# Spread the making of w_down blocks, make the first gate/up block earlier, and remake the even blocks: two FNet and GEGLU layer pairs on one core

## The chip, the cores and the metric

The kernel runs on one core of one Trainium2 chip. The metric is the device time in microseconds of one execution, the median of the runs. Lower is better.

## The reference

Activations are 2048 rows (S) by 512 columns (D); the hidden width F is 1792. The pair of layers runs twice, with the same weights:

```python
def _A_ref(x, dft_seq_re, dft_seq_im, dft_hid_re, dft_hid_im):
    a = jnp.einsum("bsd,ed->bse", x, dft_hid_re)
    b = jnp.einsum("bsd,ed->bse", x, dft_hid_im)
    y = jnp.einsum("ts,bse->bte", dft_seq_re, a) - jnp.einsum("ts,bse->bte", dft_seq_im, b)
    return y

def _B_ref(x, w_gate, w_up, w_down):
    return (_gelu(x @ w_gate) * (x @ w_up)) @ w_down

x = A_x
x = x + _A_ref(_layernorm(x), ...)
x = x + _B_ref(_layernorm(x), ...)
x = x + _A_ref(_layernorm(x), ...)
x = x + _B_ref(_layernorm(x), ...)
```

## The kernel before

**Precision.** Every float32 operand is split into a high and a low float32r part: ScalarE copies the high part (line 128), VectorE subtracts it for the low part (line 130). A product is three matmuls, high by high, high by low, low by high (lines 174 to 176), 128 by 128 weights against 128 by 512 data.

**Fewer products.** The products are done by 2 by 2 block schemes with seven products in place of eight. Their operands are sums of blocks, named A11, A12, S1 to S4 and A22; VectorE makes the sums (`plus`, line 159, and `minus`, line 156).

**Layers 0 and 2** (`mix`) are the Fourier layers. The sequence matrix comes from memory as tiles of `ws`, in four row blocks of 512 rows, numbered 0 to 3. In layer 0 the A11 and A12 products of all four row blocks come first. Then follow, for each row block, the stage S2 (24 steps: the S2, S1 and S3 products) and the stage S4 (16 steps: S4 and A22), and the hidden-matrix products: for row blocks 0 and 1 one by one, for row blocks 2 and 3 together in a pair stage after the S4 stage of row block 3. A step is one call of `six` or of the like, six matmuls. At the end of S2 `plus(v, us[b][c], one[c])` reads two PSUM banks, and the S4 stage then accumulates into the same banks.

**Layers 1 and 3** (`geglu`) are the GEGLU layers, each in two halves `w` of 1024 rows. A half runs through 14 gate/up blocks (even numbers gate, odd ones up), `up(n)` for each, seven products and so seven steps; beside them run the A11 and A12 products with w_down of the blocks already done (`beside`), then the rest of the w_down products. A gate/up block is 512 KB of raw weights `wgu`. To *make* it is to load the raw weights (one load of 256 KB, two of 128 KB, lines 1072 to 1074), take four half-wide sums, split four pieces (3.5 splits), and store the parts to memory as seven tiles `wb` of 256 KB; later halves load the stored parts. `weight_steps` gives this as a `load` and five `runs` (the sums, four divisions). Blocks in `ANEW` are never stored and are made again in each later half. A w_down block (`wdc`, parts stored as `wc`) is made in the same way by `down_weight_steps`, and comes back by the stream of loads below; there are seven, of which the first two are made in layer 0.

**Who does what when.** One list `queue` holds small pieces of work; `step()`, called once per step, takes one of them. When `queue` is empty, `step()` takes one run from `spare`, which holds the w_down blocks' runs; `slow` is taken every few steps. In layer 0 the list `chores` of a row block is put into `queue` after the S4 stage of row block 2: the loads of gate/up blocks 0 and 1, the norms of the second half of the next layer's first 1024 rows, and the making of block 0. A norm loads a row tile of x in four pieces (`x_load_mixed`, line 215), takes its mean and variance on ScalarE and GpSimd (lines 549 to 554), normalizes it (line 579) and transposes it (line 670). Loads of `ws` and of stored parts are a stream: `take()` gives the next operand and loads and splits ahead of it, as far as the tiles in SBUF allow.

**Space and order.** SBUF is 93 slots of 128 by 512 floats, given out oldest first: a load into a slot waits until the last reader of what was there is done. The order of the instructions on each engine comes from a scheduler that starts from the order in which the program is written and moves instructions ahead of others where its own timing says so. On the chip every engine's queue runs in that order; loads are on SP's queue, stores on GpSimd's.

Of the kernel before, what the change touches and what calls it, by code (L numbers as in the profile page):

```python
# [18 lines left out]
NF = F // P  # L19
# [4 lines left out]
GELU_A = math.sqrt(2.0 / math.pi)  # L24
GELU_C = 0.044715
AHEAD = 7
MORE = 8
RAW = 6
WARM = 11
# [5 lines left out]
PACE = 9, 3  # L35
SKEW = 2, 1
NSLOT = 93
DOWN_FROM = 1
BEFORE = 2
ANEW = 3, 5, 7, 9  # L40
FORE = {0: 4, 2: 4}
MADE = 5
KEEP22 = {0: (), 2: ()}
PAIRED = {0: (2,), 2: (0, 2)}
# [19 lines left out]
def fnet_geglu(ctx: ExitStack, tc: tile.TileContext, x_in, ws, wh, whc, wgu, wdc, out):  # L64
# [226 lines left out]
    stream = {"loaded": 0, "split": 0, "used": 0, "more": 0}  # L291
# [24 lines left out]
        parts[n] = items[n][2](*raws.pop(n))  # L316
        stream["split"] += 1

    def brought_near():
        n = stream["used"]  # L320
        while stream["split"] < len(items):
            at = stream["split"]
            _, _, make, need = items[at]
            if too_far(at) or make is not whole and at > n + AHEAD + stream["more"]:
                break
            if make is not whole and need and need not in cs and at > n:
                break
            split_next()

    def take():  # L330
        n = stream["used"]
        brought_near()
        stream["used"] += 1
        return parts.pop(n)

# [96 lines left out]
    NP = NF // 2  # L432
# [63 lines left out]
                    items.append((F32R, (piece_of(wdd, k, name),), whole, near))  # L496


    queue, slow, spare, deferred, steps_done, pace = [], [], [], [], [0], [PACE[0]]

    def step():
        if queue:
            run = queue.pop(0)
            if run is not None:
                run()
        elif spare:
            spare.pop(0)()
            if len(spare) == 2 and down_making:
                load, runs = down_making.pop(0)
                load()  # L510
                spare.extend(runs)
        steps_done[0] += 1
        if deferred:
            deferred.pop(0)()
        elif slow and steps_done[0] % pace[0] == 0:
            slow.pop(0)()
# [217 lines left out]
    def mix(layer):  # L734
# [6 lines left out]
        def other_chores(b):  # L741
            if b == NB - 3:
                norms, others = block_steps(layer + 1, 0)
                later.update(norms=norms[NT:], fetches=others[:ND], others=others[ND:])
                return norms[:NT]
            if b == NB - 2:
                weights = [weight_steps(n) for n in range(2)] if layer == 0 else []
                norms = later.pop("norms")
                later["others"] += weights[1][1] if weights else []
                return [run for load, _ in weights for run in (load,)] + norms + (weights[0][1] if weights else [])  # L750
            return later.pop("others") if b == NB - 1 else []

        def hid_groups(b, groups):
# [91 lines left out]
        chains, sides, us, xrows, later = {}, {}, {}, {}, {}  # L845

        def plain_hid(b):
            return b not in PAIRED[layer] and b - 1 not in PAIRED[layer]
# [12 lines left out]
        def s2(b):  # L861
            last, fore = b == NB - 1, b < FORE[layer]
            if b == 0:
                lend("z")
                lend("x")
                if layer == 0:
                    pace[0] = PACE[1]
                    slow.extend(made_ahead())
            chain, one, three = chains.pop(b), [ps8.get() for _ in range(2)], [ps8.get() for _ in range(2)]
            sides[b] = one, three  # L870
            if last:
                queue.extend([run for fetch in later.pop("fetches") for run in (None, None, None, None, fetch)])
            for i, k in skewed(3):
                if plain_hid(b) and i == 0 and k == ROWS_AT:
                    xrows[b] = [x_load(layer, b * NT + n) for n in range(NT)]
                if b and fore and i == 0 and k == (0 if layer else BACK_AT):
                    cs.update({(0, c): fetched((layer, b, c, "sum"), True) for c in range(2)})
                if i == 0:
                    six(chain, "T2", k, False, k == NK - 1)
                elif i == 1:  # L880
                    six(one, "T1", k, k == 0, k == NK - 1, "T12" if last else None)
                else:
                    six(three, "T3", k, k == 0, k == NK - 1)
                if k < NK - 1:
                    continue
                if i == 0:
                    us[b] = [copied(p, True) for p in chain]
                    ps8.put(*chain)
                    if b in xrows:
                        seeds[b] = [seeded(t) for t in xrows[b]]  # L890
                        sb.put(*xrows.pop(b))
                for c in range(2):
                    if i == 1:
                        v = cs[1, 2 + c] = sb.get(own=True)
                        plus(v, us[b][c], one[c])
                        if plain_hid(b):
                            nc.scalar.activation(one[c], v, AF.Copy)
                    elif i == 2:
                        plus(cs[1, 2 + c], cs[1, 2 + c], three[c])
# [202 lines left out]
    def down_weight_steps(k):  # L1102
        return weight_steps(k, wdc, wdd)
# [10 lines left out]
            runs += [*todo[:2], *([after[0]] if after else []), *todo[2:]]  # L1114
        return runs

    down_making = []

    def piece_here(n, i, tiles):
        p = wparts.setdefault(n, {})  # L1120
# [24 lines left out]
    def geglu(w, layer):  # L1145
# [11 lines left out]

        making = {}
        if layer == 1 and w == 0:
            down_making.extend(down_weight_steps(k) for k in range(BEFORE, NP))  # L1160
            load, runs = down_making.pop(0)
            load()
            spare.extend(runs)
            making.update((n, weight_steps(n)) for n in range(2, NF))
            making[2][0]()
        else:
            making.update((n, weight_steps(n)) for n in ANEW)


        chain, side, c11, u, w4 = {}, {}, {}, {}, {}  # L1170
# [27 lines left out]

        def up(n):
            if layer == 1 and w == 0:  # L1200
                brought_near()
            if n + 3 in making:
                making[n + 3][0]()
            if n + 2 in making:
                first_run, *runs = making[n + 2][1]
                queue.extend([lambda: (first_run(), runs[0]()), *runs[1:]])
            product(n, chain[n], "S2", "T2", False, True)
            u[n] = copied(chain[n])
            down = beside(n)
            next(down, None)  # L1210
            side[n] = ps8.get()
            product(n, side[n], "S1", "T1", True, True)
            w4[n] = copied(side[n])
            next(down, None)
            first(n + 1)
            product(n, chain[n], "S3", "T3", False, True)
            v = w4.pop(n)
            plus(v, v, chain[n])
            finished(n, 1, 1, v)
            sb.put(v)  # L1220
            next(down, None)
            product(n, side[n], "S4", "B22", False, True)
            v = u.pop(n)
            plus(v, v, side[n])
            ps8.put(side.pop(n))
            finished(n, 0, 1, v)
            sb.put(v)
            next(down, None)
            second(n + 1)
            product(n, chain[n], "A22", "T4", False, True)  # L1230
            ps = chain.pop(n)
            if n % 2 == 0:
                v = copied(ps)
                finished(n, 1, 0, v)
                sb.put(v)
            else:
                finished(n, 1, 0, ps)
            ps8.put(ps)
            for _ in down:
                pass  # L1240
# [3 lines left out]
        def pair_combined(k):  # L1244

            b11, b12, b21, b22 = h4[k] = [h.pop((2 * k + i, part)) for i in range(2) for part in range(2)]
            minus(b11, b12, b11)
            minus(b12, b22, b12)
            bs["A12", k] = split_slot(b21)
            if k < MADE:  # L1250
                second_made(k)
                fourth_made(k)
# [64 lines left out]
                if name == "S4":  # L1317
                    rows_done(layer, w * 2 + 1)

        def beside_at(j):  # L1320

            if layer == 1 and w == 0:
                return DOWN_FROM + j * (NF - DOWN_FROM) // (NF - 1)
            return j + 1

        def beside(n):

            for j in range(NF - 1):
                if beside_at(j) != n:
                    continue  # L1330
                k, other = divmod(j, 2)
                if other:
                    pair_combined(k)
                    yield from down_product("A12", k)
                    continue
                if k == NP - 1:
                    load_turned(layer, w * 2)
                bs["A11", k] = split_slot(h[2 * k, 0])
                yield from down_product("A11", k)

        straight = []

# [39 lines left out]
        if w == 0:  # L1382
            norms, others = block_steps(layer, 1)
# [194 lines left out]
```

## Time and profile before

| | before |
|---|---|
| runs shown | 1596.65, 1597.31, 1597.11 us; median 1597.11 us |
| profiled execution | 1594.51 us, span 1592.7 us |
| TensorE busy | 1579.0 us, 6976 matmuls |
| VectorE, ScalarE, GpSimd busy | 1256.5, 926.1, 247.9 us |
| granted clock, mean | 0.997 |
| moved | 405.02 MB, mean 254 GB/s |

The span runs from the first to the last instruction; what lies around it is 1.8 us. Layer 0 takes the span up to about 397 us, its third row block the stretch from 245 to 299 and its fourth that from 299 to 359; the first half of layer 1 begins at about 397. Rows of the profile name an instruction by engine, line of the kernel, operation, tiles written and read, and times are microseconds from the span's start; names such as `s`, `p` and `wide` are slots, PSUM banks and the wide tile, without their numbers. A number in brackets is the time for which the engine was idle just before, with what ended it.

### The profile page before, as it was taken

The page shows a single profiled execution, that of the slowest core. Times are in us where ns is not written, and L with a number is a line of the kernel's source. Part 1 is how long each engine was busy: PE and PEld are TensorE (multiplying, and loading weights), DVE is VectorE, ACT ScalarE, POOL GpSimd, SP SyncE. Part 2 cuts the span into 40 slices and gives each one's busy share as a digit, 9 for nine tenths or more (in the row PEclk, how much of TensorE's full clock was granted, in tenths as well). Part 3 has the DMA queues.
Part 4 walks back from the last instruction along what each step waited for, and adds up shares of the span by engine and source line. Part 5 has one row for each costly group of instructions (what it writes and reads, how often), then busy time and mean ns, then how long its engine had stood idle before and what let it go on. Part 6 is the DMA issues. An engine that isn't in the chain of part 4 may idle for free.

```text
span 1592.7 us, 23054 instructions
## 1 busy us (share of the span) xinstructions
PE 1579.0 (99%) x6976; PEld 1306.1 (82%) x6976; DVE 1256.5 (79%) x2222; ACT 926.1 (58%) x1780; POOL 247.9 (16%) x441
## 2 busy tenths in 40 slices
PE   9999999999999999999999999999999999999998
PEld 7888888878877888888888888888888888888887
DVE  8999989899988797545879988779996547864475
ACT  7866676366687653645869534557557445544351
POOL 2252221021554101100031000012002000000001
PEclk9999999999999999999999999999999999999999
DMA  9999888789999899753976785789998666894463
GB/s 363 324 350 387 303 294 286 240 278 288 316 319 317 249 311 267 223 154 94 349 264 224 252 219 178 245 269 313 277 311 219 198 193 208 299 247 138 131 198 80
DMA packets 253181, 405.02 MB, mean 254 GB/s; under 512 B 32193, under 2 KB 95425, under 8 KB 252033
## 3 DMA queue, kind: packets, MB, share of 16 engines
q1 hardware_dynamic: 227600, 322.79, 64.7%
q0 software_dynamic: 23024, 79.97, 14.1%
q8 instruction: 55, 0.90, 0.2%
q10 hardware_dynamic: 2432, 0.79, 0.2%
q14 instruction: 70, 0.57, 0.1%
HBM read 324.53 MB, written 78.91 MB: 253 GB/s over the span
## 4 chain that ended last, share of the span: by engine, by line
PE 93%; DMA 2%; ACT 2%; DVE 1%; SPq 1%; issue 1%; POOL 0%; DVEq 0%; ACTq 0%; POOLq 0%
PE p L174 31%; PE p L176 31%; PE p L175 31%; ACT s L128 1%; DMA t<-wide 1%; DMA s<-ws 1%; DMA s<-x 1%; SPq L215 0%; DVE s L130 0%; ACT s L579 0%; DMA s<-wb 0%; ACT junk L551 0%; DVE s L156 0%; DVE s L159 0%; ACT junk L549 0%
## 5 line engine op out<-in xcount | busy, mean ns | idle before, releaser
L175 PE MATMUL p<-s,s 128*128 128x512 f32 (+1 forms) x2318 | 898.2, 388 | 0.0
L176 PE MATMUL p<-s,s 128*128 128x512 f32 (+1 forms) x2318 | 885.8, 388 | 0.0
L174 PE MATMUL p<-s,s 128*128 128x512 f32 (+1 forms) x2318 | 870.6, 389 | 7.5 <-ACT s L128 4.0
L128 ACT ACTIVATE s<-s 128x512 fp32r<-128x512 f32 (+1 forms) x936 | 524.0, 607 | 283.8 <-DVE s L156 104.2
L130 DVE TENSOR_TENSOR s<-s,s 128x512 fp32r<-128x512 f32 (+1 forms) x936 | 583.7, 660 | 80.4 <-ACT s L128 77.0
L174 PEld LDWEIGHTS p<-s,s 128*128 128x128 f32 x2318 | 435.9, 188 | 101.1 <-ACT s L128 9.0
L175 PEld LDWEIGHTS p<-s,s 128*128 128x128 f32 x2318 | 436.3, 188 | 89.3
L176 PEld LDWEIGHTS p<-s,s 128*128 128x128 f32 x2318 | 435.7, 188 | 89.9 <-DVE s L152 0.2
L156 DVE TENSOR_TENSOR s<-s,s 128x512 f32<-128x512 f32 (+1 forms) x475 | 278.8, 604 | 2.4
L159 DVE TENSOR_TENSOR s<-s,p 128x512 f32<-128x512 f32 (+1 forms) x212 | 141.5, 676 | 160.2 <-PE p L176 142.7
L163 ACT ACTIVATE s<-p 128x512 f32<-128x512 f32 x236 | 137.3, 594 | 109.5 <-PE p L176 97.4
L1142 ACT ACTIVATE s<-s 128x512 f32<-128x512 f32 x84 | 53.0, 630 | 61.0 <-DVE s L159 60.7
L250 POOL DMA_DIRECT2D x<-wide x20 | 13.1, 663 | 427.2 <-DVE wide L159 263.8
L1142 ACT ACTIVATE s<-p 128x512 f32<-128x512 f32 x28 | 16.7, 598 | 82.1 <-PE p L176 81.6
L1156 DVE TENSOR_TENSOR s<-s,p 128x512 f32<-128x512 f32 x56 | 38.2, 683 | 31.3 <-PE p L176 30.9
L159 DVE TENSOR_TENSOR s<-s,s 128x512 f32<-128x512 f32 (+1 forms) x82 | 46.3, 565 | 13.6 <-DMA s<-ws 9.4
L169 ACT ACTIVATE p<-p 128x512 f32<-128x512 f32 x62 | 36.2, 583 | 35.8 <-PE p L176 27.4
L579 ACT ACTIVATE s<-s,shift,rstd 128x512 f32<-128x512 f32 x60 | 47.9, 808 | 8.1 <-POOL shift L554 4.1
L287 POOL DMA_DIRECT2D wb<-s x60 | 33.2, 555 | 83.4 <-ACT s L128 68.3
L151 ACT ACTIVATE s<-s 128x512 fp32r<-128x512 f32 x50 | 30.8, 626 | 23.6 <-PE p L176 9.3
L1156 DVE TENSOR_TENSOR s<-s,s 128x512 f32<-128x512 f32 x56 | 38.5, 688 | 1.2
L552 POOL TENSOR_SCALAR rstd<-rstd 128x1 f32<-128x1 f32 x44 | 14.8, 336 | 154.4 <-ACT junk L551 153.8
(97 smaller groups left out, 573.5 us busy)
## 6 DMA issues: line engine op xcount, KB each, us to landing
s<-ws SPq DMA_DIRECT2D x377, 256.0 KB, 5.1
s<-wb SPq DMA_DIRECT2D x210, 256.0 KB, 4.6
s<-wc SPq DMA_DIRECT2D x196, 256.0 KB, 4.6
s<-wp SPq DMA_DIRECT2D x84, 256.0 KB, 4.1
wb<-s POOLq DMA_DIRECT2D x70, 256.0 KB, 5.8
wc<-s POOLq DMA_DIRECT2D x49, 256.0 KB, 6.2
xwide<-x SPq DMA_DIRECT2D x44, 256.0 KB, 7.8
s<-x SPq DMA_DIRECT2D x36, 256.0 KB, 5.3
```

What stands on the lines that cost most here:

```text
L128: nc.scalar.activation(hi, src, AF.Copy)
L130: nc.vector.tensor_tensor(lo, src, f32(hi), op=ALU.subtract)
L156: nc.vector.tensor_tensor(out, a, b, op=ALU.subtract)
L159: nc.vector.tensor_tensor(out, a, b, op=ALU.add)
L163: nc.scalar.activation(v, src, AF.Copy)
L169: nc.scalar.activation(ps, src, AF.Copy)
L174: nc.tensor.matmul(ps, ah, bh, start=start, stop=False, skip_group_check=True)
L175: nc.tensor.matmul(ps, ah, bl, start=False, stop=False, skip_group_check=True)
L176: nc.tensor.matmul(ps, al, bh, start=False, stop=stop, skip_group_check=True)
L579: nc.scalar.activation(z, x, AF.Identity, bias=shift, scale=rstd)
L1142: nc.scalar.activation(t, g, AF.Gelu_apprx_tanh)
L1156: nc.vector.tensor_tensor(t, t, v, op=ALU.mult)
```

## The change

The making of gate/up block 0 is put into `queue` at the start of the S2 stage of row block 2, with six empty steps between its parts; after that stage's S4 the norms come first, then the load of block 1. `spare` and `brought_near` go away. In layer 1's first half the w_down blocks 2 to 6 are loaded in `up(1)`, `up(3)`, ... `up(9)` and their runs put into `queue` at `up(2)`, `up(4)`, ... `up(10)`, ahead of the runs of the gate/up block. `ANEW` becomes 2, 4, 6, 8, so that the first of them is loaded raw before the first gate/up block of a half.

```diff
-DOWN_FROM = 1
-ANEW = 3, 5, 7, 9
+WEIGHT_GAP = 6
+ANEW = 2, 4, 6, 8
...
-    def brought_near():
+    def take():
         n = stream["used"]
         while stream["split"] < len(items):
...
-    def take():
-        n = stream["used"]
-        brought_near()
         stream["used"] += 1
         return parts.pop(n)
...
     def step():
         if queue:
...
-        elif spare:
-            spare.pop(0)()
-            if len(spare) == 2 and down_making:
-                load, runs = down_making.pop(0)
-                load()
-                spare.extend(runs)
...
             if b == NB - 2:
-                weights = [weight_steps(n) for n in range(2)] if layer == 0 else []
                 norms = later.pop("norms")
-                later["others"] += weights[1][1] if weights else []
-                return [run for load, _ in weights for run in (load,)] + norms + (weights[0][1] if weights else [])
+                if layer:
+                    return norms
+                load, runs = weight_steps(1)
+                later["others"] += runs
+                return [*norms, load]
...
+            if layer == 0 and b in PAIRED[layer]:
+                load, runs = weight_steps(0)
+                queue.extend([load, *[None] * WEIGHT_GAP, *[at for run in runs for at in (run, *[None] * WEIGHT_GAP)]])
...
         if layer == 1 and w == 0:
-            down_making.extend(down_weight_steps(k) for k in range(BEFORE, NP))
-            load, runs = down_making.pop(0)
-            load()
-            spare.extend(runs)
             making.update((n, weight_steps(n)) for n in range(2, NF))
-            making[2][0]()
         else:
             making.update((n, weight_steps(n)) for n in ANEW)
+        if 2 in making:
+            making[2][0]()
...
         def up(n):
             if layer == 1 and w == 0:
-                brought_near()
+                k, odd = divmod(n + 3, 2)
+                if not odd and BEFORE <= k < NP:
+                    down_making[k] = down_weight_steps(k)
+                    down_making[k][0]()
+                if n % 2 == 0 and n // 2 + 1 in down_making:
+                    queue.extend(down_making.pop(n // 2 + 1)[1])
             if n + 3 in making:
                 making[n + 3][0]()
```

`beside` is written anew with the same places for the w_down products (one after each gate/up block but the first). Each engine and each queue has as many instructions as before; the lines of the changed file are 5 to 11 lower.

Two places in the order. The first is VectorE at the end of the S2 stage of row block 3, in layer 0. Line 159 with a PSUM bank `p` as input is the sum that frees the banks for S4; `s_4102` is the low part of the first weights of S4. Before:

```order
L156 TENSOR_TENSOR s_4138<-s_4138,s_3769 128x512
L130 TENSOR_TENSOR s_4220<-s_4115,s_4219 128x512
L159 TENSOR_TENSOR s_4182<-s_4134,p_3786 128x512
L159 TENSOR_TENSOR s_4184<-s_4136,p_3787 128x512
L130 TENSOR_TENSOR s_4206<-s_4098,s_4205 128x512
L130 TENSOR_TENSOR s_4233<-s_4138,s_4232 128x512
L670 STREAM_TRANSPOSE wide<-s_4036 128x16x32
L159 TENSOR_TENSOR s_4182<-s_4182,p_3788 128x512
L159 TENSOR_TENSOR s_4184<-s_4184,p_3789 128x512
L130 TENSOR_TENSOR s_4102<-s_4009,s_4101 128x512
```

The same place after the change, where `s_4116`, `s_4133`, `s_4160` and `s_4185` are the low parts of the first weights of S4 (`s_4133` stands four rows ahead of this piece):

```order
L130 TENSOR_TENSOR s_4116<-s_4030,s_4115 128x512
L130 TENSOR_TENSOR s_4172<-s_4076,s_4171 128x512
L130 TENSOR_TENSOR s_4091<-s_3841,s_4090 128x512
L130 TENSOR_TENSOR s_4160<-s_4064,s_4159 128x512
L130 TENSOR_TENSOR s_4185<-s_4088,s_4184 128x512
L156 TENSOR_TENSOR s_4112<-s_4112,s_3753 128x512
L130 TENSOR_TENSOR s_4201<-s_4100,s_4200 128x512
L156 TENSOR_TENSOR s_4156<-s_4156,s_3800 128x512
L130 TENSOR_TENSOR s_4238<-s_4129,s_4237 128x512
L159 TENSOR_TENSOR s_4194<-s_4152,p_3817 128x512
L130 TENSOR_TENSOR s_4214<-s_4112,s_4213 128x512
L159 TENSOR_TENSOR s_4196<-s_4154,p_3818 128x512
```

The low parts for S4 moved from behind the sums that read PSUM to ahead of them, and the transpose left this piece.

The second place is SP's queue in the first half of layer 1, around the gate/up blocks 2 to 4. Line 215 is a row tile of x for a norm, four issues each; `s_5258`, `s_5260` and `s_5261` are raw weights of gate/up block 5. Before:

```order
L304 DMA s_5256<-wc_102 128x512
L1072 DMA s_5258<-wgu 128x512
L1073 DMA s_5260<-wgu 128x256
L215 DMA s_5058<-x_2_91 32x512 x4
L215 DMA s_5063<-x_2_91 32x512 x4
L215 DMA s_5068<-x_2_91 32x512 x4
L215 DMA s_5230<-x_2_91 32x512 x4
L1074 DMA s_5261<-wgu 128x256
L215 DMA s_5420<-x_3_92 32x512 x4
L1073 DMA s_5387<-wgu 128x256
```

After the change, where block 5 is `s_5179`, `s_5181` and `s_5182`, and `s_5330` is the first load of block 6:

```order
L1069 DMA s_5182<-wgu 128x256
L1069 DMA s_5053<-wgu 128x256
L304 DMA s_5209<-wc_102 128x512
L1067 DMA s_5179<-wgu 128x512
L1068 DMA s_5181<-wgu 128x256
L1067 DMA s_5323<-wdc 128x512
L1068 DMA s_5325<-wdc 128x256
L1067 DMA s_5330<-wgu 128x512
L215 DMA s_5093<-x_2_91 32x512 x4
L215 DMA s_5098<-x_2_91 32x512 x4
L215 DMA s_5103<-x_2_91 32x512 x4
```

All of block 5 moved ahead of the rows of x, twelve issues of which now stand together, and the rest of block 6 (`s_5332`, `s_5333`) behind them.

More of the change, by code (lines that the diff above doesn't have):

```diff
@@ L496, in fnet_geglu @@
                     items.append((F32R, (piece_of(wdd, k, name),), whole, near))
-    queue, slow, spare, deferred, steps_done, pace = [], [], [], [], [0], [PACE[0]]
+    queue, slow, deferred, steps_done, pace = [], [], [], [0], [PACE[0]]
     def step():
@@ L1115, in made_ahead @@
         return runs
-    down_making = []
+    down_making = {}
     def piece_here(n, i, tiles):
@@ L1318, in ended @@
                     rows_done(layer, w * 2 + 1)
[L1320 to L1324, printed above, removed]
         def beside(n):
[L1328 to L1335, printed above, removed]
+            k = (n - 1) // 2
+            if n % 2:
                 if k == NP - 1:
@@ L1338, in beside @@
                 bs["A11", k] = split_slot(h[2 * k, 0])
-                yield from down_product("A11", k)
+                return down_product("A11", k)
+            if n:
+                pair_combined(k)
+                return down_product("A12", k)
+            return iter(())
         straight = []
```

## The prediction

> **What bounds the kernel now.** I read the page's parts 1 and 2 first, then who TensorE waited for, then stretches of equal length, and last the instructions around each gap.
>
> ```profile
> span 1592.7 us, 23054 instructions
> PE 1579.0 (99%) x6976; PEld 1306.1 (82%) x6976; DVE 1256.5 (79%) x2222; ACT 926.1 (58%) x1780; POOL 247.9 (16%) x441
> ...
> PE p L174 <- ACT s L128: 4.0, 4, 2.3
> PE p L174 <- DVE s L130: 2.5, 1, 2.5
> ```
>
> TensorE is the bound, and its idle time is not all it loses: matmul ends are modelled, so I count matmuls per stretch instead. The next rows are windows: length, busy time and count of each engine, then granted clock, DMA share, GB/s.
>
> ```profile
> 92.00:169.00 77.00, 77.00 (x341) 63.62 (x340) 73.04 (x130) 49.25 (x91) 28.40 (x48) 1.00 0.96 355
> ...
> 100.00:115.00 15.00, 15.00 (x67) 12.39 (x67) 15.00 (x27) 8.40 (x16) 8.00 (x14) 1.00 1.03 389
> 330.00:345.00 15.00, 12.05 (x45) 9.16 (x44) 14.77 (x26) 12.16 (x24) 4.59 (x8) 0.89 0.95 318
> 445.00:460.00 15.00, 11.90 (x44) 9.02 (x44) 15.00 (x29) 14.09 (x33) 12.14 (x22) 0.89 1.04 310
> 490.00:505.00 15.00, 14.42 (x63) 11.39 (x62) 14.24 (x27) 10.02 (x21) 6.88 (x13) 1.00 0.80 284
> 505.00:520.00 15.00, 14.52 (x64) 11.73 (x63) 11.15 (x23) 8.96 (x17) 7.49 (x15) 1.00 0.98 323
> 1240.00:1255.00 15.00, 14.92 (x66) 12.01 (x65) 8.19 (x15) 7.82 (x17) 1.61 (x5) 1.00 0.53 186
> 1400.00:1415.00 15.00, 15.00 (x68) 12.43 (x67) 9.76 (x17) 6.60 (x13) 0.00 (x0) 1.00 1.08 254
> ```
>
> An unbroken stretch of 77 us holds 341 matmuls, 340 steps, so one step is 0.2265 us; 15 us hold 67 or 68, say 67.5. Missing are 22.5 at 330 (call it A: 5.1 us), 23.5 at 445 (B: 5.3), 4.5 at 490 (C: 1.0), 3.5 at 505 (D: 0.8) and 1.5 at 1240 (E: 0.3). That is 12.5 us, and after the first 30 us I found no other place where matmuls stand apart. A and B hold 10.4 of it. Part of each is clock, granted 0.89 in both windows:
>
> ```profile
> 334.04 0.39 PE L176 MATMUL p<-s,s 128*128 128x512 f32 x1
> 336.89 0.73 PE L174 MATMUL p<-s,s 128*128 128x512 f32 x2 [2.46 <-DVE s L130]
> 338.11 0.50 PE L174 MATMUL p<-s,s 128*128 128x512 f32 x1 [0.48 <-DVE s L159]
> ...
> 340.42 0.63 PE L176 MATMUL p<-s,s 128*128 128x512 f32 x1
> 340.85 0.63 PE L174 MATMUL p<-s,s 128*128 128x512 f32 x1
> ...
> 342.10 0.39 PE L175 MATMUL p<-s,s 128*128 128x512 f32 x1
> ```
>
> After the gap from 334.04 to 336.89 matmuls start 0.43 apart (340.42 to 340.85), until 342.10; B looks alike. The many loads, splits and stores elsewhere cost TensorE nothing; only these five places count.
>
> **What ends A.** A is the start of the fourth row block's S4 stage. Rows of ScalarE, the chain, VectorE:
>
> ```profile
> 328.66 0.81 ACT L579 ACTIVATE s<-s,shift,rstd 128x512 f32<-128x512 f32 x1 [1.37 <-POOL shift L554]
> 329.50 3.68 DMA s<-ws
> 333.18 0.68 DVE L156 TENSOR_TENSOR s<-s,s 128x512 f32<-128x512 f32 x1
> 334.38 1.27 DVE L159 TENSOR_TENSOR s<-s,p 128x512 f32<-128x512 f32 x2
> 336.78 0.70 DVE L670 STREAM_TRANSPOSE wide<-s 128x512 f32<-128x512 f32 x1
> 338.58 1.27 DVE L130 TENSOR_TENSOR s<-s,s 128x512 fp32r<-128x512 f32 x2
> ```
>
> A row of x was normalized at 328.66; only then was its slot free, the sequence-matrix load into it landed at 333.18, and VectorE, in order, stood at that subtraction. Behind it were the two sums that read PSUM (334.38), which free the banks S4 writes, then a transpose, and the low parts of S4's first weights. VectorE was busy 32.00 of 33 us before that (next fence), so nothing was caught up.
>
> **What ends B.** The fifth gate/up block's raw weights stand on SP's queue behind sixteen issues of x rows:
>
> ```profile
> 428.07 12.37 SPq L215 DMA_DIRECT2D s<-x  x16
> 440.54 0.40 SPq L1074 DMA_DIRECT2D s<-wgu  x1
> ...
> 444.05 0.43 DVE L159 TENSOR_TENSOR s<-s,s 128x256 f32<-128x256 f32 x1 [0.99 <-DMA s<-wgu]
> ...
> 449.32 0.50 PE L174 MATMUL p<-s,s 128*128 128x512 f32 x1 [2.30 <-ACT s L128]
> ```
>
> The 16 issues take 12.37 us, the last quarter of the block is asked for at 440.54, its sums begin at 444.05, the split follows behind the statistics of five x rows, and TensorE resumes at 449.32.
>
> **The change part by part.** It takes away no instruction and adds none: every engine and queue has as many as before; only the order moves.
>
> *Block 0 of gate/up, moved into the third row block.* It carries three loads on SP, four half-wide sums and 3.5 splits on VectorE, 3.5 on ScalarE, seven stores on POOL. Groups by line and shape, stores on POOL, DMA issues, and the two stages:
>
> ```profile
> L156 DVE TENSOR_TENSOR s<-s,s 128x256 f32<-128x256 f32 x140 | 56.3, 416 | 0.5
> L130 DVE TENSOR_TENSOR s<-s,s 128x512 fp32r<-128x512 f32 x857 | 555.7, 682 | 71.0 <-ACT s L128 67.7 <-PE p L176 1.5 <-DMA wp<-s 0.8
> L128 ACT ACTIVATE s<-s 128x512 fp32r<-128x512 f32 x857 | 500.4, 625 | 283.4 <-DVE s L156 103.8 <-DVE s L1156 59.3 <-PE p L176 37.2
> ...
> 328.57 1.15 POOL L287 DMA_DIRECT2D wb<-s  x2
> ...
> wb<-s POOLq DMA_DIRECT2D x70, 256.0 KB, 5.8
> s<-wgu SPq DMA_DIRECT2D x26, 256.0 KB, 4.6
> ...
> 245.00:299.00 54.00, 54.00 (x240) 44.72 (x239) 45.84 (x77) 27.19 (x49) 5.67 (x9) 1.00 0.85 272
> 299.00:332.00 33.00, 33.00 (x147) 27.32 (x146) 32.00 (x58) 21.24 (x48) 9.81 (x16) 1.00 0.83 278
> ```
>
> VectorE: 4 x 0.416 + 3 x 0.682 + 0.416 = 4.1 us; ScalarE 3 x 0.625 and a half one, about 2.3; POOL 7 x 0.58 = 4; SP 3 x 0.4. In the third row block VectorE goes from 45.84 to 50 of 54 us, 92%, against 73.04 of 77 (95%) in the stretch from 92 on that has no gap; ScalarE and POOL have room. Bytes: 0.5 MB in, 7 x 256 KB out, 2.3 MB. At 272 GB/s for a share of 0.85 that is 7.2 us of full DMA, which lifts the share over 54 us to about 0.98; the gapless row had 0.96. Nearest rows say cost 0, the upper end is one more A, 5.1. I take 0 and keep the end as a rival. The block's seven parts stay in slots: counted along the program, the fewest free slots in the third row block's S4 fall from 13 to 6, and the shortest way from a slot's release to the first matmul on its new data in the fourth row block from 101 to 91 matmuls; the pair stage has 72 and ran without a gap.
>
> *What it leaves behind.* The fourth row block loses that 4.1 us on VectorE where it was full, and the norms begin four steps earlier, ahead of block 1's load. The order shows it: the low part of S4's first weights stood seven places behind the first sum that reads PSUM, and stands nine places ahead of it; no transpose is between. The loads that feed this spot sit in slots freed by matmuls or splits, none by a norm of that batch. So of A's 5.1 I keep 0.3 (ends 0 and 5.1; nearest is the same point of the third row block, inside the unbroken 54 us at 245).
>
> *w_down blocks and the new SP order.* Five blocks, 4.1 us of VectorE each, are made either way. Before, they were made three runs per gate/up block from the first on; now five runs at every second block from the third on. With that, the fifth block's raw loads are issued ahead of the x rows: from its last load to its first matmul the order has 145 matmuls instead of 35, that is 33 us instead of 8. Landing 4.6, four sums 1.7 and a split pair 1.3 make 7.6. The smallest such distance after the change is 65 (15 us, block 2); before, one of 73 ran without a gap. Behind the x rows now stands block 6, with 110. So B goes, but in order ScalarE still takes x statistics before the copy that the next S4 product needs; I keep 0.6 (ends 0 and 5.3; C's size is nearest).
>
> *C and D* are products that wait for something made right before them, C for a split behind its multiply, D for a copy into PSUM behind a gelu:
>
> ```profile
> 499.11 0.99 PE L174 MATMUL p<-s,s 128*128 128x512 f32 x3 [0.58 <-ACT s L128]
> ...
> 511.05 0.63 ACT s L1142
> 511.68 0.50 ACT p L169
> ...
> 512.22 0.50 PE L174 MATMUL p<-s,s 128*128 128x512 f32 x1 [0.48 <-ACT p L169]
> ```
>
> Those chains stay, with somewhat fewer rows ahead: 1.2 of 1.8 kept (ends 0 and 3.6, twice as many of them). E, in the last layer, I keep whole: 0.3.
>
> *Blocks 2, 4, 6, 8 anew.* Four blocks are made and ten stored, as before; block 2 is then wanted first, 67 matmuls (15 us) after its loads, against the 7.6 worked out. Cost 0, or one gap of C's size in each of three stages, 3.0 at most; I take 0.7 for new small gaps in all. *The loads of w_down parts* are asked for at the product, not at the block's head, a dozen matmuls later with some 100 left: 0, since 23 us cover a landing of 5; without that cover each would cost a gap of C's size.
>
> Sum: 12.5 - (0.3 + 0.6 + 1.2 + 0.3 + 0.7) = 9.4 us saved. The profiled execution took 1594.51, its span 1592.7; it would take 1585.1. The median shown is 1597.11, 2.6 above it; I carry that over: 1587.7.
>
> One rule reads otherwise. The Trainium skill, "TensorE: Matmul & The Clock Gate", section "HAM oscillation — how this bites in real kernels", puts the clock's loss at idle gaps over about 3.4 us. By it the 2.85 us gap of A should have cost no clock, so the slow matmuls (0.11 of 15 us in each window, 3.3) would have another cause and stay: an estimate of 1591.0. The trace shows them right behind a shorter gap and nowhere else, so I let them go with it.
>
> **Rivals.** (1) The DMA engines fill up in the third row block and a sequence load comes late there: share 0.98 speaks for it, the gapless 0.96 and 1.03 against. One more A: 1592.8. Beside it: the Trainium skill, "DMA: Bandwidth & Descriptors", "Issuing engines are not separate DMA queues", says that transfers of SP and POOL interleave on the same 16 engines; the trace agrees as far as B fell where the share was 1.04. (2) B comes again, since twelve x issues still stand together ahead of part of block 6 and a statistic waits for its row in ScalarE's queue: 1593.0; 110 matmuls of room speak against. (3) The gaps wander, since in-order queues are nearly full (VectorE 15.00 of 15 at 445), and the saving is spent elsewhere: 1597. (4) Slower: every second gate/up block now gets nine runs for seven steps, so a block's last divisions slide into the next. If VectorE runs over four steps late (30 matmuls, 6.8 us), the next block's first product waits, five times. From 2.5 us each it is slower; at 3 each 1602.7, at B's size 1614.2. Against it: from block 5 on the order has the raw loads 89 to 146 matmuls ahead of need, and VectorE falls to 11.15 of 15 at 505.
>
> **How the numbers follow.** Forecast 0.68, (1) 0.10, (2) 0.08, (3) 0.08, (4) 0.06. A measurement of this kernel tells about 0.2%, 3.2 us, from no change: faster is below 1593.9. The forecast, (1) and (2) lie there but for about 0.03: faster 0.83, same 0.11, slower 0.06. The range starts a little below 1584.6, where all 12.5 go, since the 2.6 carried over may hold gaps too: 1584.0; it ends past (1) and (2), at 1593.5.
>
> **What would show it.** The count in the windows around A and B back at 67 or 68 with clock 1.00; the sixteen-issue train broken up; VectorE's PSUM sums at the end of that S2 within a microsecond of TensorE; the third row block at 240 matmuls in 54 us. A count under 235 there, a granted clock below 1.00 after 30 us, or waits at every second gate/up block of the first half would prove me wrong.

## The result, and the profile after

Changed, the kernel takes 1586.64 us (median of 4 runs, 1583.69 to 1587.34), beside 1597.21 us for the kernel before on the same chip (4 runs, 1596.65 to 1599.87): a ratio of 0.9924 (the two medians alone give 0.9934), 95% interval 0.9910 to 0.9939. Of the executions reported below one, of after_odd, took 1747.2 us at a granted clock of 0.851 and is left out of its row. The profiled execution took 1587.34 us. From its page, first the span, TensorE, and what TensorE waited for:

```profile
span 1585.0 us, 23089 instructions
...
PE 1575.0 (99%) x6976; PEld 1303.7 (82%) x6976; DVE 1255.7 (79%) x2222; ACT 925.8 (58%) x1780; POOL 246.8 (16%) x441
...
PE p L174 <- DVE s L159: 1.4, 2, 0.9
...
PE p L174 <- ACT s L128: 0.8, 2, 0.4
PE p L174 <- ACT p L169: 0.6, 1, 0.6
```

The wait of 2.5 us for line 130 and the longest one, 2.3 us, for line 128 are gone. The windows of A, B, C, D and E, and the third row block ahead of them (columns as before):

```profile
245.00:299.00 54.00, 54.00 (x240) 44.73 (x239) 49.44 (x85) 29.58 (x53) 10.20 (x17) 1.00 0.91 295
...
330.00:345.00 15.00, 15.00 (x68) 12.43 (x67) 15.00 (x28) 9.07 (x17) 0.00 (x0) 1.00 0.72 217
...
445.00:460.00 15.00, 15.00 (x68) 12.43 (x67) 14.19 (x27) 12.71 (x26) 10.36 (x16) 1.00 1.08 347
490.00:505.00 15.00, 15.00 (x68) 12.40 (x67) 15.00 (x32) 10.52 (x20) 9.04 (x16) 1.00 1.00 356
505.00:520.00 15.00, 15.00 (x68) 12.43 (x67) 13.85 (x27) 8.84 (x18) 8.52 (x14) 1.00 0.86 291
1240.00:1255.00 15.00, 15.00 (x68) 12.41 (x67) 8.73 (x13) 6.61 (x14) 1.66 (x5) 1.00 0.69 218
```

All five hold 68 matmuls at clock 1.00. Block 0 lies in the third row block (VectorE 45.84 to 49.44 of 54 us, share 0.85 to 0.91), which still holds 240. What is lost now lies elsewhere:

```profile
441.09 0.50 PE L174 MATMUL p<-s,s 128*128 128x512 f32 x1 [0.47 <-DVE s L159]
...
473.21 2.44 DMA wb<-s
...
475.14 0.63 ACT L539 ACTIVATE junk<-s 128x512 f32<-128x512 f32 x1 [1.15 <-DMA s<-x]
...
481.03 0.50 PE L174 MATMUL p<-s,s 128*128 128x512 f32 x1 [0.64 <-ACT p L169]
...
917.55 0.50 PE L174 MATMUL p<-s,s 128*128 128x512 f32 x1 [0.92 <-DVE s L159]
```

Added up over the spacing of 0.2267 us between matmuls, 0.77 us go at 440, 1.78 from 476 to 481 and 1.24 at 917, in layer 2. The second row is a store, from the chain of work that ended last; the third a statistic on ScalarE that waited for its row of x; TensorE felt it at 481.

### The profile page after: what moved, and what is told of

Read it like the earlier page. It is cut to its first block, busy times and chain, and to the rows that moved or that the text cites. A ratio compares the mean times of both kernels' runs of the same rounds, so it can differ in the third digit from the quotient of the medians.

```text
span 1585.0 us, 23089 instructions
## 1 busy us (share of the span) xinstructions
PE 1575.0 (99%) x6976; PEld 1303.7 (82%) x6976; DVE 1255.7 (79%) x2222; ACT 925.8 (58%) x1780; POOL 246.8 (16%) x441
## 3 DMA queue, kind: packets, MB, share of 16 engines
q0 software_dynamic: 23024, 79.97, 14.2%
HBM read 324.53 MB, written 78.91 MB: 255 GB/s over the span
## 4 chain that ended last, share of the span: by engine, by line
PE 94%; DMA 2%; DVE 2%; issue 1%; ACT 1%; SPq 0%; POOL 0%; DVEq 0%; ACTq 0%; POOLq 0%
PE p L174 31%; PE p L176 31%; PE p L175 31%; DMA s<-ws 1%; DVE s L130 1%; DMA s<-wgu 1%; DVE s L156 0%; ACT s L128 0%; DVE s L159 0%; DVE s L1151 0%; DMA wb<-s 0%; SPq L304 0%; ACT s L569 0%; SPq L237 0%; SPq L206 0%
```

## The experiments

Two theories of B were put against each other. *Requests*: the raw weights stand too late on SP's queue, behind rows of x (the prediction's reason). *Bytes*: the stores of w_down and gate/up parts crowd the DMA engines while layer 1 starts, so that loads land late whatever stands where. For A the question was which of the two moves in layer 0 removes it. All kernels are compared in three stretches; an unbroken one counts 68 (330 to 345 us, A), 156 (425 to 460, B) and 266 or 267 (465 to 525) matmuls. The kernel before, in the last two:

```profile
425.00:460.00 35.00, 31.90 (x133) 25.59 (x132) 28.31 (x54) 27.89 (x63) 20.96 (x38) 0.95 0.97 323
465.00:525.00 60.00, 58.94 (x258) 47.93 (x258) 52.71 (x102) 38.96 (x78) 27.58 (x49) 1.00 0.96 323
```

| kernel | us, median (runs) | ratio to before, 95% | A, of 68 | 425 to 460, of 156 | 465 to 525, of 267 |
|---|---|---|---|---|---|
| before | 1597.21 (4) | | 45 | 133 | 258 |
| after | 1586.64 (4) | 0.9910 to 0.9939 | 68 | 152 | 258 |
| layer0_only | 1598.67 (11) | 1.0000 to 1.0018 | 68 | 94 | 266 |
| layer1_only | 1589.69 (5) | 0.9949 to 0.9974 | 41 | 156 | 267 |
| norms_first | 1598.46 (1) | | 66 | 114 | 260 |
| block0_early | 1597.93 (1) | | 63 | 96 | 265 |
| spread_only | 1591.08 (9) | 0.9949 to 0.9975 | 35 | 156 | 258 |
| after_even_stored | 1602.34 (1) | | 68 | 144 | 229 |
| l0_fewer | 1588.01 (1) | | 68 | 139 | 267 |
| l0_x3 | 1594.98 (10) | 0.9978 to 1.0004 | 68 | 148 | 232 |
| after_odd | 1587.01 (4) | 0.9911 to 0.9950 | 68 | 149 | 267 |
| v_anew6 | 1587.03 (4) | 0.9913 to 0.9950 | 68 | 140 | 267 |
| after_x3 | 1584.52 (4) | 0.9900 to 0.9935 | 68 | 156 | 266 |
| v6_x3 | 1583.66 (4) | 0.9892 to 0.9930 | 68 | 154 | 266 |

The kernel before moves by some us from run to run (1591.3 to 1600.5 over all), and each ratio is to the kernel before as measured beside that row, so medians of different rows differ by some us without meaning; single runs are read by their traces.

**layer0_only.** The kernel before with the layer-0 part of the change alone.

```diff
+                load, runs = weight_steps(1)
+                later["others"] += runs
+                return [*norms, load]
...
+            if layer == 0 and b in PAIRED[layer]:
+                load, runs = weight_steps(0)
+                queue.extend([load, *[None] * WEIGHT_GAP, *[at for run in runs for at in (run, *[None] * WEIGHT_GAP)]])
```

> The kernel before with only the layer 0 part of the change (block 0 made in the third row block, norms ahead of block 1's load); w_down blocks, ANEW and the loads of w_down parts as before. All theories: gap A (5.1 us at 330 to 345) goes to under 0.5. Theory 1, that B is the fifth block's raw loads issued late: this order has 107 matmuls between its last load and its first product (35 before, 145 after the whole change), so B falls under 1 us and the kernel is 9 to 11 us faster than before. Rival, that B comes from the w_down blocks made three runs per gate/up block beside it: B stays at 4 to 6 us and the kernel is only 5 us faster.

A is whole, and nothing is won. Its B, from the windows and the rows on SP and TensorE:

```profile
425.00:460.00 35.00, 24.07 (x94) 18.42 (x93) 22.28 (x46) 23.29 (x54) 19.28 (x35) 0.85 0.99 308
...
425.77 15.46 SPq L216 DMA_DIRECT2D s<-x  x16
441.33 0.43 SPq L1079 DMA_DIRECT2D s<-wgu  x1
...
443.77 0.42 DVE L160 TENSOR_TENSOR s<-s,s 128x256 f32<-128x256 f32 x1 [9.19 <-DMA s<-wgu]
...
451.42 0.79 PE L175 MATMUL p<-s,s 128*128 128x512 f32 x1 [9.67 <-ACT s L164]
```

B grew to 62 missing matmuls, 14.0 us; neither theory had expected more than 6. The train of 16 issues of x rows is there again, 15.46 us long, 0.97 each, and the weights behind it came late: VectorE stood idle 9.19 us for them. So the gain of A was lost 100 us later.

**layer1_only.** The changed kernel with the layer-0 part undone (the lines above taken out, the two loads and block 0 back in `chores`).

> The changed kernel with the layer 0 part undone (block 0 made in the fourth row block, both loads ahead of the norms). All theories: A stays at 4.5 to 5.5 us, since VectorE's order there is that of before. Theory 1 (147 matmuls from the fifth block's last load to its product) and its rival both take B under 1 us; so 5 to 7 us faster than before. If the two parts only work together, under 3 us faster.

```profile
330.00:345.00 15.00, 12.62 (x41) 9.33 (x41) 14.77 (x27) 11.49 (x23) 4.59 (x8) 0.77 0.85 303
...
425.00:460.00 35.00, 35.00 (x156) 28.96 (x155) 28.90 (x55) 29.51 (x69) 17.97 (x34) 1.00 0.98 291
```

A stays and B is gone. Of the two parts, layer 0's alone is worth nothing (2.2 us slower than the median of the kernel before beside it), layer 1's 6.8, both together 10.6: they don't add.

**norms_first** and **block0_early** cut the layer-0 part in two: the norms ahead of the loads of blocks 0 and 1 with block 0 where it was, and block 0 made early with block 1's load still ahead of the norms.

```diff
-                return [run for load, _ in weights for run in (load,)] + norms + (weights[0][1] if weights else [])
+                return norms + [run for load, _ in weights for run in (load,)] + (weights[0][1] if weights else [])
```

```diff
-                return [*norms, load]
+                return [load, *norms]
```

> The kernel before with one thing changed: in the fourth row block the norms come ahead of the loads of blocks 0 and 1; block 0 is still made in that row block. If A is VectorE's load there (4.1 us of block 0), A stays at 3 us or more. If A is the slots freed late by norms, A falls under 1 us. B: 39 matmuls from the fifth block's last load to its product, as before, so theory 1 has B stay at 4 to 6 us.

> The layer 0 part of the change without its reordering of the norms: block 0 made in the third row block, block 1's load still ahead of the norms, all else as before. If A is VectorE's load, A falls under 1 us. If A is the order of norms against loads, A stays at 3 us or more. B: 107 matmuls from the fifth block's last load to its product: under 1 us by theory 1, 4 to 6 by its rival.

The window of A in the one and then in the other:

```profile
330.00:345.00 15.00, 14.84 (x66) 11.98 (x65) 13.97 (x27) 7.65 (x15) 0.86 (x2) 1.00 1.06 274
```

```profile
330.00:345.00 15.00, 14.14 (x63) 11.40 (x62) 14.67 (x26) 10.69 (x21) 0.63 (x1) 1.00 0.88 269
```

Either edit takes most of A: 0.45 and 1.11 us of 5.15 are left, so neither of the two causes that were set against each other is the only one. In both, B grew (114 and 96 of 156, 9.5 and 13.6 us), as in layer0_only and beyond what either theory had expected.

**spread_only.** layer1_only with `ANEW = 3, 5, 7, 9`: the spreading of w_down and nothing else.

> The kernel before with the spreading of the w_down blocks alone (and the SP order that goes with it): block 0 of gate/up is made where it was, and blocks 3, 5, 7, 9 are made anew. Compared with the layer-1 part whole (7.0 us faster than before, A 5.9 us kept, B, C, D gone). If the spreading carries B, C and D, this gives 1589 to 1592 and about 10 stores or fewer in the 45 us from layer 1's start, TensorE losing less than 1 us there. If the choice of blocks 2, 4, 6, 8 (block 2 not stored, block 3 stored) carries part of it, there are more stores there and B comes back with 2 to 5 us: 1592 to 1596.

B is gone with 156 of 156, and the total is within 1.4 us of layer1_only's; 2.0 us went between 476 and 484, as in the changed kernel. The spreading carries the gain, the choice of blocks doesn't; but it moves the stores, the work of VectorE and ScalarE and the order of the loads all at once, so this run does not say which of them B needed. **after_odd**, the changed kernel with `ANEW = 3, 5, 7, 9`, says the same from the other side, 0.4 us from the changed kernel. The first 45 us of layer 1 hold 7 stores of w_down and 13 of gate/up parts in both, so it does not test the bytes:

> The changed kernel with blocks 3, 5, 7, 9 made anew, as before the change, and not 2, 4, 6, 8. Beside the stages' cost of each choice, which I put at nothing, this moves one block's seven stores (block 2) into the time when w_down's first and the x rows run. By theory 2 the 45 us from layer 1's start hold about 7 stores more than the changed kernel's 7, and TensorE loses 0.5 to 3 us more: 1587 to 1590. If the choice does nothing: within 1.5 us of the changed kernel.

**after_even_stored.** Bytes added. The kernel stores blocks 4 and 6 once more than the changed one; that is 14 stores, not the 21 named below, as block 2 was still not stored.

```diff
-                if place is wblocks and n in ANEW:
+                extra = place is wblocks and n in (2, 4, 6) and (n, i) not in stored_too
+                stored_too.add((n, i))
+                if place is wblocks and n in ANEW and not extra:
```

> The changed kernel, but gate/up blocks 2, 4 and 6 are also stored once, as they are made in layer 1's first half: 21 stores of 256 KB more on GpSimd's queue, which nothing loads again; VectorE, ScalarE, TensorE and the loads do exactly the work of the changed kernel. Theory 2 (stores beside the x rows fill the DMA engines, x issues on SP stretch, the statistics and raw weights behind them come late): the changed kernel has 7 stores in the 45 us from layer 1's start and x issues of 0.42 us in the median, the layer-0 part alone 19 and 1.04 us; with about 14 stores more there the issues go to 0.7 to 1.0 us, the DMA share of the third 15 us to 0.95 or more, and TensorE loses 3 to 10 us there, the total going up by as much (1590 to 1597). Rival (it is the VectorE and ScalarE work of making w_down blocks beside the first gate/up blocks, not their bytes): issues stay below 0.6 us or stretch without harm, TensorE loses less than 1.5 us there more than in the changed kernel, total within 2 us of it.

Windows, the chain, VectorE and TensorE:

```profile
465.00:525.00 60.00, 54.88 (x229) 42.81 (x228) 46.02 (x93) 33.44 (x67) 28.56 (x51) 0.97 0.83 292
566.00:581.00 15.00, 12.77 (x49) 10.10 (x48) 13.51 (x23) 4.94 (x10) 0.00 (x0) 0.89 1.06 314
...
462.93 16.63 DMA s<-wgu
...
479.59 0.42 DVE L159 TENSOR_TENSOR s<-s,s 128x256 f32<-128x256 f32 x1 [4.99 <-DMA s<-wgu]
...
481.60 0.79 PE L174 MATMUL p<-s,s 128*128 128x512 f32 x1 [2.68 <-DVE s L1153]
```

The sign was that of bytes, the size beyond both: over the even spacing it loses 15.6 us more than the changed kernel, of which only 2.0 at B's place, 6.7 from 460 to 525, 4.0 at 573 and 1.8 at 1240, later than expected. A load of raw gate/up weights that went out at 462.93 landed 16.63 us later, and VectorE stood idle 4.99 us for it. No engine computes more here.

One step can be compared cleanly. From 395 us to the end of the train of twelve x issues SP's queue has the same loads in the same order in both kernels. Its train, and then the share of the 16 DMA engines' time that q0 took from 418 to 431 us (packets, MB, share), first here and then in the changed kernel. q0 is the queue of GpSimd's stores: in the changed kernel it moved 79.97 MB, where 78.91 MB in all were written to memory.

```profile
418.31 11.96 SPq L215 DMA_DIRECT2D s<-x  x12
...
q0 software_dynamic: 1188, 3.90, 81.1%
```

```profile
q0 software_dynamic: 585, 1.88, 37.7%
```

There are 11 stores in these 13 us, and 4 in the changed kernel. The same twelve issues took 11.96 us instead of 8.75, and their rows landed 5.3 us after the issue in the median instead of 3.4. So more stores did make SP's issues and the landings behind them longer. Behind the train the scheduler put the rows and the weights out in another order, so the later losses are not the bytes' alone; and what the run does not separate there is the bytes from the slots that the stores hold until they have landed.

**l0_fewer.** Bytes taken away. layer0_only with other blocks made anew, so that 2, 4 and 6 are not stored while layer 1 starts.

```diff
-ANEW = 3, 5, 7, 9
+ANEW = 2, 3, 4, 5, 6
...
             making.update((n, weight_steps(n)) for n in ANEW)
+            making[2][0]()
```

> The layer-0 part alone (B 14.25 us, total 1598.7), with gate/up blocks 2, 3, 4, 5, 6 made anew in the later stages in place of 3, 5, 7, 9, so that blocks 2, 4 and 6 are not stored while layer 1 starts: 21 stores of 256 KB fewer there. The w_down blocks are made at the same steps as in the layer-0 part alone, with the same work on VectorE and ScalarE. If the bytes of the stores make B, B falls below 5 us (more likely 1 to 3) and the total to 1587 to 1592. If the making of w_down blocks beside the first gate/up blocks makes it (VectorE, ScalarE, the order), B stays above 10 us and the total above 1595.

```profile
425.00:460.00 35.00, 32.95 (x139) 26.76 (x138) 31.79 (x66) 30.56 (x73) 21.77 (x37) 0.95 1.01 289
```

B fell from 62 missing matmuls to 17, with every w_down block made at the step where layer0_only makes it: 1588.0 us without any spreading. From SP's queue where the x rows go out, and the share of q0 from 420 to 437 us:

```profile
420.07 5.42 SPq L216 DMA_DIRECT2D s<-x  x9
425.60 0.36 SPq L1079 DMA_DIRECT2D s<-wgu  x1
...
427.01 2.38 SPq L216 DMA_DIRECT2D s<-x  x5
...
q0 software_dynamic: 479, 1.54, 23.6%
```

In layer0_only q0 took more than three times that share while its train went out, from 425 to 442 us:

```profile
q0 software_dynamic: 1503, 4.89, 77.3%
```

The issues of x rows shortened to 0.60 and 0.48 us each. But the train itself is broken up too: the scheduler, with fewer stores to place, put loads of raw weights between the x rows. Fewer stores and another order of requests came together here, and this run does not part them.

**l0_x3.** Requests changed and bytes kept: layer0_only with each row of x in layer 1's second 1024 rows asked for one norm earlier.

```diff
-                for k in range(i if i == 0 or i + NT == end and not w else i + 2, min(i + 3, end)):
+                more = 3 if w and layer == 1 else 2
+                for k in range(i if i == 0 or i + NT == end and not w else i + more, min(i + more + 1, end)):
```

> The layer-0 part alone (B 14.25 us, total 1598.7, 19 w_down stores in the 45 us from layer 1's start), with each row of x in layer 1's second set of rows asked for one norm earlier; the w_down blocks stay where they were, and every store with them. If B is the late request of x rows (sixteen issues in one train ahead of raw weights, statistics that hold ScalarE), it falls below 3 us and the total to 1585 to 1589: the spreading of w_down is then not needed. If the bytes of the stores make it whatever the order of requests, B stays above 8 us and the total above 1592.

The second window, the chain, ScalarE, TensorE:

```profile
465.00:525.00 60.00, 54.10 (x232) 44.27 (x231) 48.45 (x94) 34.98 (x68) 25.23 (x46) 0.94 0.86 301
...
466.68 13.43 DMA s<-wdc
...
486.62 1.50 ACT L580 ACTIVATE s<-s,shift,rstd 128x512 f32<-128x512 f32 x2
...
490.87 0.80 PE L175 MATMUL p<-s,s 128*128 128x512 f32 x1 [5.90 <-ACT s L164]
```

B's stretch is nearly whole (148 of 156), though a train of sixteen x issues still stands there (from 424.77, 13.11 us), and 7.9 us go 40 us later: the chain leads through a load of raw w_down weights that took 13.43 us to land, a load of gate/up weights issued only then, VectorE behind it, and ScalarE, where two norms (486.62) stand ahead of the copy that TensorE waits for. Asking earlier moved the loss; some 10 of 14 us stayed. The total is 3 us under the median of the kernel before, which the interval (0.9978 to 1.0004) does not tell from no change.

**after_x3, v_anew6, v6_x3.** The same edit on the changed kernel; six blocks anew (`ANEW = 2, 3, 4, 5, 6, 8`, 14 stores fewer and 42 loads of stored parts fewer); both.

> The changed kernel with each row of x in layer 1's second set of rows asked for one norm earlier (three ahead, not two), and nothing else. The changed kernel loses 1.87 us at 476 to 481 us behind a statistic that waits for its row, and 0.77 us at 440. If the request is late, these go: 1 to 2.5 us less than the changed kernel. If the slot or the full DMA engines hold the row, nothing is gained (within 1 us) or 1 to 3 us lost, since one more slot is taken.

> The changed kernel with six blocks made anew (2, 3, 4, 5, 6, 8) and so eight stored, not ten. If bytes of stores and of loads are what still costs the first half of layer 1 (a gap of 1.87 us where a statistic waits for an x row whose slot a store kept), that gap goes: 1 to 2 us less than the changed kernel, 1584 to 1586. If VectorE's extra work in the three later stages (two more blocks made each time, about 8 us of VectorE in some 250 us) makes new gaps, 1 to 4 us more: 1588 to 1591.

> Blocks 2, 3, 4, 5, 6, 8 anew, which lost 3.8 us in one place at 441 to 447 us, where a statistic on ScalarE waits for its row of x 8 us after the row was asked for; and each row of x in layer 1's second set of rows asked for one norm earlier (three ahead, not two). If the late row is what cost those 3.8 us, they go, and the total is 1583 to 1584. If the row is late because its slot is freed late, or the DMA engines are full (share 1.11 there), asking earlier brings nothing or shifts the wait: 1586 to 1589.

after_x3, its first stretch; the second holds 266:

```profile
425.00:460.00 35.00, 35.00 (x156) 29.00 (x155) 30.44 (x61) 31.40 (x74) 24.73 (x44) 1.00 1.04 334
```

Here, with the stores spread, the earlier request is enough: both of layer 1's gaps close in the trace, 2.1 us on the median, though its runs (1582.5 to 1586.2) overlap the changed kernel's. v_anew6 closed the one at 476 and opened another, 3.7 us, although it has fewer stores: a statistic stood 2.98 us for a row of x, with the DMA share at 1.11 from 435 to 450. So the number of stores does not decide alone:

```profile
444.78 0.63 ACT L539 ACTIVATE junk<-s 128x512 f32<-128x512 f32 x1 [2.98 <-DMA s<-x]
```

v6_x3 closed that too, and is the fastest of all, 1583.66 us; it and after_x3 lie within 1 us, and their runs overlap.

## Why the prediction was right, and where not

*A* (kept 0.3, measured 0.0). The prediction gave two reasons, the 4.1 us taken off a full VectorE and the norms four steps earlier. norms_first has only the second, block0_early only the first, and each takes most of A (4.7 and 4.0 of 5.15 us); only both together take all of it.

*The third row block* (taken as 0 between 0 and 5.1): 240 matmuls, VectorE 49.44 us for 50 forecast, the share 0.91 for 0.98. Rival (1) is out.

*B* (kept 0.6, measured 0.77). The number is close by luck, and the reason was half of one. The 0.6 was kept for x statistics on ScalarE ahead of a copy; at 441 TensorE waited for a sum of VectorE. The prediction put B on the place of the fifth block's raw loads, 35 matmuls of room before and 145 after. layer0_only left the w_down blocks as they were and lost 14 us, with 107 matmuls of room by its expectation; l0_x3 asked for rows of x earlier and lost most of it elsewhere; l0_fewer removed stores and brought B down to 3.9 us. So room in the order alone did not remove the lateness, and the stores have a large part in it: SP's issues of x rows took 0.77 us each before and 0.97 in layer0_only, and 14 stores more lengthened the changed kernel's train from 0.73 to 1.00 each. In two kernels loads of raw weights took 13 and 17 us, where the prediction reckoned with 4.6. What the spreading did was to move w_down's stores out of the first 45 us of layer 1: 17 there before, 19 in layer0_only, 7 after. How much of B's end is these stores and how much the new order of the loads, no run separates, since every edit moved the order too.

*C and D* (kept 1.2, measured 0.0). Both windows are whole in layer1_only and in spread_only, but in layer0_only and l0_fewer as well, where the w_down blocks stay where they were. So the term was too large, and no single edit is shown to end them. *E* (kept 0.3) is gone without any edit to its place, and in layer0_only as well: it wanders.

*New small gaps* (0.7, measured 3.0: 1.78 and 1.24; the expectations put the first at 1.87). This is the mis-sized term. The first is the mechanism of rival (2), a statistic that waits for its row in ScalarE's queue, 30 us later and a third of the size. The second, in layer 2, is in eight of the twelve other kernels tried (1.3 to 2.0 us) and in neither the kernel before nor the other four; the order there is the same before and after. VectorE stood idle 3.92 us ahead of a sum at 915.60, and 2.57 us ahead of the same sum in the kernel before; beside it a load took 6.4 us to land, before 5.0. Why the loads land later there stays open.

*The sum.* 12.5 less 3.1 kept made 9.4; by the gaps 3.8 stayed and 8.7 went, and the last matmul starts 8.5 us earlier. The end behind it took 0.8 us more, so the span fell 7.7, from 1592.7 to 1585.0. The 2.6 us by which the profiled run before lay under its median were carried over, and the profiled run after lies 0.7 above its own. The execution was forecast 2.2 us too short (1585.1 for 1587.34, 1.7 of it span) and the step to the median 3.3 too long; they pull opposite ways, and 1587.7 stands 1.1 from 1586.64. That they cancel is luck: the total is better than its parts. Rival (4), nine runs per even block, shows nowhere: no gap returns at every second block. Rival (3), a saving spent elsewhere, is what the layer-0 part does when it stands alone.

*The clock.* A's slow matmuls went with its gap, as the prediction held against the rule of the Trainium skill ("TensorE: Matmul & The Clock Gate", "HAM oscillation — how this bites in real kernels"), by which the prediction's estimate of the total was 1591.0. The runs narrow it; from v_anew6 and from l0_fewer, matmuls behind a gap:

```profile
444.79 0.39 PE L176 MATMUL p<-s,s 128*128 128x512 f32 x1
447.03 0.50 PE L174 MATMUL p<-s,s 128*128 128x512 f32 x1 [1.86 <-ACT s L163]
...
449.51 0.63 PE L175 MATMUL p<-s,s 128*128 128x512 f32 x1
449.93 0.63 PE L176 MATMUL p<-s,s 128*128 128x512 f32 x1
```

```profile
1118.78 0.39 PE L177 MATMUL p<-s,s 128*128 128x512 f32 x1
1120.93 0.50 PE L175 MATMUL p<-s,s 128*128 128x512 f32 x1 [1.76 <-DVE s L160]
...
1123.12 0.39 PE L175 MATMUL p<-s,s 128*128 128x512 f32 x1
1123.36 0.39 PE L176 MATMUL p<-s,s 128*128 128x512 f32 x1
```

The first gap was 2.25 us from start to start, and the matmuls two and a half us later start 0.42 us apart; the second was 2.15 us, and they go on at 0.23 or 0.24. After the first 30 us of these fourteen traces slow matmuls follow every gap from 2.25 us on and none from 1.5 to 2.15 us, so the page's limit of about 3.4 us did not hold here; whether the length alone decides is not shown.

## What to carry to other kernels

Read a stretch of late landings as one budget of DMA time. Here, asking for rows earlier moved the gap while the stores stood close together (l0_x3), and runs with the stores spread or fewer lost less (spread_only, l0_fewer), though their order of loads changed as well, and v_anew6 shows that fewer stores can still open a new gap. Test the parts of a change alone before crediting them: here one part saved time in its own stretch and lost it 100 us later until the other was there too. Once the stores are spread, asking for rows one step earlier is the cheap next edit (after_x3).

## What the hardware showed that was not expected

A load's landing stretched far beyond the median of its group: 16.63 us for 128 KB of raw gate/up weights in after_even_stored and 13.43 us for 256 KB of raw w_down weights in l0_x3. The medians of their groups from 390 to 480 us (count, KB each, median us) were 5.0 and 8.9:

```profile
s<-wgu SPq DMA_DIRECT2D x9, 128.0 KB, 5.0
```

```profile
s<-wdc SPq DMA_DIRECT2D x3, 256.0 KB, 8.9
```

SP's own issues stretched as well: a quarter row of x (64 KB) took 0.97 us in the train of sixteen of layer0_only, and 0.73 in the changed kernel's train of twelve:

```profile
418.62 8.75 SPq L215 DMA_DIRECT2D s<-x  x12
```

The Trainium skill ("DMA: Bandwidth & Descriptors", "Issuing engines are not separate DMA queues") calls the time to initiate a DMA usually small beside the DMA itself. In layer0_only 16 such issues held SP's queue for 15.46 us, where one transfer took 4.6 us from issue to landing in the median (425 to 442 us): one issue was a fifth of a transfer, and the train of them over three times one.

```profile
s<-x SPq DMA_DIRECT2D x16, 64.0 KB, 4.6
```
